# The seam between attention and the expert layer: where the first early tile's scatter, the experts' ranking and a weight block stand, and a new table of keys

## The chip, the cores and the metric

The kernel runs on one core of a Trainium2 chip. The metric is the device time in microseconds from one launch; before and after are compared on medians of several runs. TensorE is called PE, VectorE DVE, ScalarE ACT, GpSimd POOL and SyncE SP, as in the profile. Each engine works through its own queue strictly in order.

## What is computed

Linear attention for 8 batches of 8 heads, normalised per head, and behind it a layer of 8 experts of which each token uses one. A token is kept while its expert has places.

```python
kv = einsum('bhsd,bhse->bhde', k, v); out = einsum('bhsd,bhde->bhse', q, kv)    # 8 x 8 x 576 x 64
x = out / sqrt(mean(out ** 2, -1) + 1e-6) * g_norm                              # -> 4608 tokens x 512
logits = x @ w_gate; e = argmax(logits); gate = softmax(logits)[e]
h = maximum(x_e @ w1[e], 0)                                                     # 512 -> 1024
out[token] = gate * (h @ w2[e])                                                 # 1024 -> 512
```

## The kernel before

**Stages.** The attention part (about 0 to 150 us) works batch by batch: products for `kv` and for the output on PE, squares and normalisation, routing, and a write of the token rows to the tensor `x_dram`. Behind the fifth batch an early part begins: the expert that leads by then gets its weights loaded and its first 384 tokens (`EARLY`) gathered, and its first products are done beside the rest of the attention. Behind the last batch `finish` (L1343) reads the table of tokens per expert from PSUM (`read_table`, `tab_sb`, L1141), makes the row numbers of the first expert's other tokens (`sources_of_first`, `gi_rest`, L1154), and ranks the other experts by their load (`rank_steps`, L1110: compare, rank, turn, keep; the last gives `perm_i`). Then each expert has a budget of slots (704, 672, 640, 624, 592, 576, 560, 512), in tiles of 128 rows. The first expert has 320 slots left behind its early ones.

**One expert.** Its rows come by indirect gathers from `x_dram` that POOL issues (`xg`, L457), are scaled to `xm`, turned so that the 512 features lie on partitions, and split into two float16 parts (`xs`: high and low). For the first expert PE turns them (`xp`, L477), ACT and DVE copy the parts (L713, L485); for the others ACT and POOL or DVE make the pair of parts (`pair`, L491, L495) and SP issues a DMA transpose (L501). Weights are loaded by SP (`raw`, L345, four pieces of 512 KB a matrix), their maximum is taken on DVE (`am`, L361), and they are split into high and low float16 parts by ACT (L395) and DVE (L401). The hidden layer is 8 tiles `hp` of three products each (x high by w high, x low by w high, x high by w low; L551); its relu is split again (`hb`, ACT L556, DVE L559). The second product `yp` (L597) takes 24 matmuls for each tile of 128 rows: hidden high by w2 high, hidden high by w2 low, hidden low by w2 high. ACT scales it by the gate (`ysb`, L632) and POOL scatters it to the output by an indirect DMA (L637).

**The order of the work.** It is not written out by hand and not left to the compiler: while the kernel is built, class `Plan` lists the operations with assumed durations (`op`, L118) and `place` (L127) puts them on the engines one by one. Of the operations that an engine could begin soonest it takes the one with the lowest key, and of equal keys the one with the lowest number. Keys are 10 for each expert in turn (`KEY`) with small steps inside, lower for what is urgent, plus an entry for an operation's number from the table `NUDGE`, if there is one. The first plan holds the attention and early part, the second (`NUDGE[1]`) the rest. Operations are numbered as the code makes them. In the second plan 1 to 18 belong to the two early tiles that are left, 19, 26 and 33 are the three gathers of the first expert's rest (128, 128 and 64 rows), 40 to 104 its products, 105 the copy `next_i` that tells SP the second expert, 106 to 154 the second expert's rows, 155 to 228 its weights, and so on.

Of the early tokens' three output tiles the first is made in the first plan (`EARLY_TILES` = 1), scatter included; the two others (`range(EARLY_TILES, NHI)`, L1761) in the second, beside the gathers. SP's loads of the second expert's w1 wait for `next_i`, which waits for the ranking and for the three gathers:

```python
before = [op(("P", 0.12), lambda e: nc.gpsimd.tensor_copy(next_i, perm_i[0:1, 0, 1:2]),
             [early["rank"]] + sent, -KEY / 2)]
```

## Time and profile before

| | |
|---|---|
| median of 3 runs | 559.38 us (556.1, 559.38, 563.11) |
| profiled execution | 556.98 us device time, span of the instructions 555.1 us, mean granted clock 0.985 |
| busy | PE 520.3 us (94%), DVE 394.1 (71%), ACT 252.7 (46%), POOL 150.9 (27%) |
| data moved by DMA | 102.58 MB, mean 185 GB/s |

PE's share is the first thing to read: what the engine with 94% does not do is what an order of the work can still give. The busy share is a mean over two very different parts, so it has to be cut by stretch. A number in brackets such as `[2.56 <-ACT xs L713]` at a line of the timeline is the idle time of the engine before that line and what ended it.

### The profile page before, as it was taken

How to read it: one execution, taken by the hardware profiler on the slowest of the kernel's cores; microseconds unless marked ns; L12 is line 12 of the kernel's file. 1: busy time of each engine (PE TensorE's matmuls, PEld its weight loads, DVE VectorE, ACT ScalarE, POOL GpSimd, SP SyncE). 2: the span in 40 equal slices, each digit the busy share in tenths (PEclk: the TensorE clock that was granted, in tenths of full speed). 3: DMA queues.
4: the chain of work that ended last, by engine and by line, in shares of the span. 5: the costliest groups of instructions: out<-in, count | busy, mean ns of one | idle time of the engine just before them, and what ended most of it. 6: DMA issues, size and time to landing. Idle time of an engine off the chain costs nothing.

```text
span 555.1 us, 12017 instructions
## 1 busy us (share of the span) xinstructions
PE 520.3 (94%) x4599; PEld 344.2 (62%) x4599; DVE 394.1 (71%) x1041; ACT 252.7 (46%) x506; POOL 150.9 (27%) x173
## 2 busy tenths in 40 slices
PE   4989797898996999999999999999999999999995
PEld 4878695876544666546754675667468648745442
DVE  3389679989967679869868899779778785751200
ACT  1667475698413346237246282264246165212210
POOL 6001002612356553243404320220503151002011
PEclk9999798899999999999999999999999999999998
DMA  8999999744256979778619538747529341001010
GB/s 272 358 356 360 392 380 368 252 144 182 98 155 249 226 242 264 154 151 266 159 49 322 144 92 280 139 144 259 142 65 305 115 119 38 1 20 58 0 40 32
DMA packets 78019, 102.58 MB, mean 185 GB/s; under 512 B 43222, under 2 KB 51414, under 8 KB 76932
## 3 DMA queue, kind: packets, MB, share of 16 engines
q1 hardware_dynamic: 69600, 70.43, 43.3%
q0 software_dynamic: 7776, 31.30, 16.0%
q8 instruction: 38, 0.62, 0.5%
q14 instruction: 25, 0.20, 0.1%
q10 hardware_dynamic: 580, 0.02, 0.1%
HBM read 73.13 MB, written 20.61 MB: 169 GB/s over the span
## 4 chain that ended last, share of the span: by engine, by line
PE 19%; issue 18%; DMA 11%; DVE 3%; POOL 1%; ACT 1%; POOLq 0%; DVEq 0%
DMA out_dram<-ysb,si 11%; PE hp L551 11%; PE yp L597 6%; DVE am L361 2%; PE yp L612 1%; ACT w2h L395 1%; POOL xg L457 1%; DVE hb L559 1%; POOL out_dram L637 0%; POOL gt L472 0%; POOLq L1740 0%; POOLq L637 0%; DVE xm L465 0%; ACT hb L556 0%; DVE w2l L401 0%
## 5 line engine op out<-in xcount | busy, mean ns | idle before, releaser
L551 PE MATMUL hp<-xs,w1h 128*128 128x320 f16 (+6 forms) x896 | 134.6, 300 | 5.7 <-ACT xs L713 2.6
L597 PEld LDWEIGHTS <-hb 128*128 128x128 f16 x840 | 81.2, 98 | 93.4 <-issue 0.7
L597 PE MATMUL yp<-w2h,hb 128*128 128x512 f16 x544 | 127.1, 379 | 0.3 <-ACT ysb L632 0.2
L551 PEld LDWEIGHTS <-w1h 128*128 128x128 f16 x960 | 93.3, 98 | 46.9 <-issue 7.8
L637 POOL DMA_INDIRECT out_dram<-ysb,si x41 | 46.3, 1130 | 238.1 <-ACT ysb L632 180.8
L361 DVE TENSOR_REDUCE am<-raw 128x1 f32<-128x512 f32 x120 | 75.3, 677 | 12.5 <-DMA raw<-in_moe_w_dram 12.4
L556 ACT ACTIVATE hb<-hp 128x320 f16<-128x320 f32 (+7 forms) x64 | 40.6, 636 | 84.8 <-PE hp L551 70.9
L559 DVE SCALAR_TENSOR_TENSOR hb<-hp,hb 128x320 f16<-128x320 f32 (+7 forms) x64 | 47.2, 737 | 35.8 <-ACT hb L556 35.6
L551 PE MATMUL hp<-xs,w1l 128*128 128x320 f16 (+6 forms) x448 | 71.5, 300 | 0.0
L632 ACT ACTIVATE ysb<-yp,ysc 128x512 f32<-128x512 f32 (+5 forms) x40 | 27.4, 684 | 94.2 <-PE yp L597 90.9
L597 PE MATMUL yp<-w2l,hb 128*128 128x512 f16 x272 | 64.7, 379 | 0.0
L551 PEld LDWEIGHTS <-w1l 128*128 128x128 f16 x480 | 46.9, 98 | 19.4
L457 POOL DMA_INDIRECT xg<-x_dram,gi x35 | 37.1, 1061 | 34.5 <-DVE xm L465 19.8
L861 PE MATMUL op<-kv_bd,qt 128*128 128x144 f32 x256 | 44.2, 316 | 1.6 <-ACT qt L713 1.1
L401 DVE SCALAR_TENSOR_TENSOR w2l<-raw,sw,w2h 128x512 f16<-128x512 f32 x64 | 44.8, 743 | 0.5 <-ACT w2h L395 0.4
L401 DVE SCALAR_TENSOR_TENSOR w1l<-raw,sg,w1h 128x512 f16<-128x512 f32 x64 | 45.0, 746 | 0.0
L491 ACT CAST pair<-xm 128x512 f16<-128x512 f32 (+5 forms) x35 | 21.3, 615 | 46.1 <-DVE xm L465 24.1
L395 ACT ACTIVATE w1h<-raw,sg 128x512 f16<-128x512 f32 x60 | 38.8, 711 | 7.0 <-DVE sg L390 7.0
L395 ACT ACTIVATE w2h<-raw,sw 128x512 f16<-128x512 f32 x62 | 40.1, 713 | 1.0 <-DVE sw L331 1.0
L861 PEld LDWEIGHTS op<-kv_bd,qt 128*128 128x128 f32 x256 | 37.8, 210 | 3.8 <-ACT qt L713 1.8
L772 PE MATMUL a<-v_sb,k_sb 64*64 64x64 f32 x576 | 23.6, 233 | 9.2 <-DMA v_sb<-in_v_dram 7.4
L772 PEld LDWEIGHTS a<-v_sb,k_sb 64*64 64x64 f32 x576 | 20.7, 145 | 12.9 <-issue 11.6
(250 smaller groups left out, 634.6 us busy)
## 6 DMA issues: line engine op xcount, KB each, us to landing
raw<-in_moe_w_dram SPq DMA_DIRECT2D x64, 512.0 KB
k_sb<-in_k_dram SPq DMA_DIRECT2D x16, 576.0 KB
v_sb<-in_v_dram SPq DMA_DIRECT2D x16, 576.0 KB
x_dram<-o_sb POOLq DMA_DIRECT2D x8, 1152.0 KB
q_sb<-in_q_dram SPq DMA_DIRECT2D x16, 512.0 KB
x_dram<-o_sb POOLq DMA_DIRECT2D x8, 144.0 KB
q_sb<-in_q_dram SPq DMA_DIRECT2D x32, 32.0 KB
out_dram<-ysb,si POOLq DMA_INDIRECT x41
```

The lines of the kernel that those rows point to most:

```text
L361: nc.vector.tensor_reduce(out=am()[:, p:p + 1], in_=raw[:, sl(p)], axis=AX.X, op=ALU.max, apply_absolute_value=True)
L395: nc.scalar.activation(wh[:, sl(p)], raw[:, sl(p)], AF.Copy, scale=z["s"])
L401: nc.vector.scalar_tensor_tensor(out=wl[:, sl(p)], in0=raw[:, sl(p)], scalar=z["s"], in1=wh[:, sl(p)], op0=ALU.mult, op1=ALU.subtract)
L457: nc.gpsimd.indirect_dma_start(out=self.xg[i][0:n], out_offset=None, in_=x_dram[0:self.rows, :], in_offset=bass.IndirectOffsetOnAxis(ap=se ...
L551: nc.tensor.matmul(self.view(hp)[:, u], lhsT=w[:, c, j * P:(j + 1) * P], rhs=x[:, c, u * hw:(u + 1) * hw], start=(t == 0 and c == 0), stop ...
L556: nc.scalar.activation(self.out(self.hh, j), self.view(hp), AF.Relu)
L559: nc.vector.scalar_tensor_tensor(out=self.out(self.hl, j), in0=self.view(hp), scalar=0.0, in1=self.out(self.hh, j), op0=ALU.max, op1=ALU.s ...
L597: nc.tensor.matmul(yp[0:n, 0:DM], lhsT=h[:, j, o:o + n], rhs=w[:, j, :], start=(m == 0), stop=(m == len(self.terms) - 1))
L632: nc.scalar.activation(self.ysb[0:n], yp[0:n, 0:DM], AF.Copy, scale=self.ysc[0:n, i:i + 1])
L637: nc.gpsimd.indirect_dma_start(out=out[:, :], out_offset=bass.IndirectOffsetOnAxis(ap=self.sidx[0:n, col:col + 1], axis=0), in_=ysb[0:n], ...
L772: nc.tensor.matmul(banks[g].t[rows[u], half * D:(half + 1) * D], lhsT=kh.t[rows[g], u, c * D:(c + 1) * D], rhs=vh.t[rows[g], u, c * D:(c + ...
L861: nc.tensor.matmul(y, lhsT=qt.t[:, i * P:(i + 1) * P], rhs=kv2[:, half * HH + i], start=True, stop=True)
```

## The change

Four edits and a new table. (1) `second` gets a list `kept`: the scatter of the first early tile is not issued in the first plan but kept, and issued in the second with key -5, behind the three gathers of the first expert's rest (`first_sent`). Two empty operations stand in its place, so that the numbers of the others stay. (2) `finish` lets the copy of the experts' counts and the four steps of the ranking depend on `early["cut"]`, the operation that makes `gi_rest`. (3) `Gemm2` gets `low_last`, set for the early expert's tiles: the block hidden high by w2 low comes third instead of second, and `second` names the dependences in that order (`r < 0`). (4) `NUDGE[1]` is replaced, 35 entries by 397. The table of the first plan stays.

```diff
@@ -80,10 +80,46 @@
-    {3: 0.6, 26: 0.6, 99: -8.8, 110: 0.7, 149: -7.4, 289: 2.9, 377: 8.6, 436: -5, 478: 0.6, 506: -2.6, 572:
-     6.1, 590: 1.6, 594: 5.7, 633: 3.6, 678: 6.1, 691: 12.4, 716: 9.4, 726: 3.2, 783: 2.3, 795: 4.8, 809:
...
+    {10: -4.3, 36: -0.3, 57: 4.2, 91: -3.2, 99: -7.1, 102: 0.2, 108: 1.4, 109: 1.4, 110: 1.2, 111: 1.4, 112:
...
+     144: 1.4, 145: 1.4, 146: 1.4, 147: 1.4, 148: 1.4, 149: 1.4, 150: 1.4, 151: 1.4, 152: 1.4, 153: 7.5, 154:
+     7.5, 155: 7.5, 156: 7.5, 157: 7.5, 158: 7.5, 159: 5.2, 160: 5.2, 161: 5.2, 162: 5.2, 163: 5.2, 164: 5.2,
+     165: -2.2, 166: 5.2, 167: 7.5, 168: 7.5, 169: 7.5, 170: 7.5, 176: 6.1, 177: 6.1, 178: 6.1, 179: 6.1, 180:
...
+     224: -18.2, 232: -5.3, 233: 1.7, 259: 8.4, 261: 2.4, 263: -1.3, 274: 0.9, 373: 1.9, 374: -2.9, 377: 8.6,
+     383: -2.9, 399: -2.5, 448: -0.1, 455: 1.2, 457: -1.5, 495: 2.2, 503: -1.5, 506: -0.9, 510: 1.9, 511: 1.9,
...
+     -1.7, 808: 2.4, 823: -3.5, 836: 5.6, 840: 8, 858: -2.6, 861: -3.4, 862: -3.4, 863: -3.4, 864: -3.4, 865:
...
+     1445: -1.8, 1455: -1.3, 1463: -0.3, 1467: 0.3, 1468: 0.7, 1496: -5.6, 1500: 1.5, 1501: -12.3, 1524: 2.8,
+     1543: -0.8, 1547: -5.8, 1556: -6.9, 1564: -6.9, 1565: -6.9, 1566: -6.9, 1567: -8.1, 1571: 7.9})
@@ -573,13 +609,14 @@
     class Gemm2:
 
 
-        def __init__(self, pool, ws, g, gt, sidx, s0, s1, bufs=3):
+        def __init__(self, pool, ws, g, gt, sidx, s0, s1, bufs=3, low_last=False):
             self.pool, self.g, self.gt, self.sidx, self.s0, self.bufs = pool, g, gt, sidx, s0, bufs
             self.w = [w.rearrange("p (j d) -> p j d", j=KF) for w in ws[2:4]]
             self.tiles = spans(s0, s1)
             self.ysc = pool.tile([P, NHI], F32, name="ysc")
             hh, hl = g.hh, g.hl
-            self.terms = [(h, w, j) for h, w in ((hh, self.w[0]), (hh, self.w[1]), (hl, self.w[0])) for j in range(KF)]
+            pairs = [(hh, self.w[0]), (hh, self.w[1]), (hl, self.w[0])]
+            self.terms = [(h, w, j) for h, w in (pairs[::2] + pairs[1:2] if low_last else pairs) for j in range(KF)]
 
         def scales(self, scale):
             c0 = 0
@@ -1080,12 +1117,12 @@
         writes.append(ws)
         lasts[b] = ws + [ent, acc]
 
-    def count(dst, key):
+    def count(dst, key, behind=None):
 
         cp = misc[:, 64:64 + E]
         o = op(("T", 0.05), lambda e: nc.tensor.matmul(cp, lhsT=ones16, rhs=tot_acc, start=True, stop=True), accs[-1:], FIRST)
         readers.setdefault("acc", []).append(o)
-        return op(("V", 0.1), lambda e: nc.vector.tensor_copy(dst, cp), [o], key)
+        return op(("V", 0.1), lambda e: nc.vector.tensor_copy(dst, cp), [o, behind], key)
 
     def distinct(cnt):
         d = sm.tile([P, E], F32, name="dist")
@@ -1259,7 +1296,7 @@
             lows.append(op(("V", 0.61), lambda e, i=i, xp=xp: st["rows"].low(i, xp.t), [a], low, (), (xp, hold)))
         return st, hold, fetched, (gates, highs, lows)
 
-    def second(r, st, hh, hl, w2, scaled, hid, w_hold, sl_hold, s0, s1, bank, tiles=range(NHI), key=None):
+    def second(r, st, hh, hl, w2, scaled, hid, w_hold, sl_hold, s0, s1, bank, tiles=range(NHI), key=None, kept=None):
 
         key = KEY * r if key is None else key
         urgent = key - KEY
@@ -1277,8 +1314,9 @@
                         st["g2"].products(i, yp.t, c, c + 4)
 
                     js = range(c % KF, c % KF + 4)
-                    after = [(hl if c >= 2 * KF else hh)[j] for j in js] + [scaled, o]
-                    after += [w2[KF <= c < 2 * KF][j] for j in js] if w2 else []
+                    block = (0, 2, 1)[c // KF] if r < 0 else c // KF
+                    after = [(hl if block == 2 else hh)[j] for j in js] + [scaled, o]
+                    after += [w2[block == 1][j] for j in js] if w2 else []
                     o = op(("T", 0.86), product, after, k, (yp,), (hid, w_hold))
             else:
                 yt = new("ysb")
@@ -1303,9 +1341,16 @@
                 yh.t = st["g2"].out(i, yp.t)
 
             o = op(("A", 0.58), out_, [o], urgent, (yh,), (yp,))
+            if kept is not None:
+                kept.append((o, lambda e, i=i, yh=yh: st["g2"].write(i, yh.t)))
+                o = op(("S", 0.01), None, o if isinstance(o, list) else [o], key)
+                o = op(("S", 0.01), None, [o], key)
+                continue
             o = op(("P", 1.05), lambda e, i=i, yh=yh: st["g2"].write(i, yh.t), [o], key, (), (yh, sl_hold))
             o = op(("D", 0.73), None, [o], key, (), (yh,))
         return o
+
+    kept_writes = []
 
     def early_products():
         st = early["st"] = {}
@@ -1331,12 +1376,12 @@
             hl.append(op(("V", 0.07 + EARLY / 960), lambda e, j=j, hp=hp: st["g1"].low(j, hp.t), [a], LOW, (), (hp,)))
 
         def scales(e):
-            st["g2"] = Gemm2(ep, wsets[0], st["g1"], early["x"]().gt, early["si"], 0, EARLY, 2)
+            st["g2"] = Gemm2(ep, wsets[0], st["g1"], early["x"]().gt, early["si"], 0, EARLY, 2, True)
             st["g2"].scales(y_scale(*[early["z", i]["e"] for i in range(2)]))
 
         early["scaled"] = op(("V", 1.2), scales, gates + hh[:1] + list(early["w", 1][0].values()), LOW)
         second(-1, st, hh, hl, early["w", 1], early["scaled"], Hold(None), Hold(None), Hold(None), 0, EARLY,
-               ("op", lambda: bank("op")), range(EARLY_TILES), LOW + 2)
+               ("op", lambda: bank("op")), range(EARLY_TILES), LOW + 2, kept_writes)
 
     cnt_all = cst.tile([P, E], F32, name="cnt_all")
 
@@ -1355,9 +1400,9 @@
         early["cut"] = op(("V", 0.65), cut, [t], key)
         early["sources"] = op(("V", 0.2), lambda e: sources(), [t], key + 0.1)
         early["cut2"] = op(("V", 0.8), cut2, [t], key + 0.3)
-        o = count(cnt_all, key)
+        o = count(cnt_all, key, early["cut"])
         for long, f in rank_steps(cnt_all):
-            o = op(("V", long), lambda e, f=f: f(), [o], key + 0.2)
+            o = op(("V", long), lambda e, f=f: f(), [o, early["cut"]], key + 0.2)
         early["rank"] = o
 
     tiles = {0: load(0)}
@@ -1751,6 +1796,7 @@
            range(EARLY_TILES, NHI))
     st, xs_hold, sent, (gates, xh, xl) = rows(lambda: (early["gi0"], None), EARLY, BUDGET[0], N, [early["cut"]], -KEY, -KEY / 2,
                                               mo, None, lambda: psx.tile([P, 512], F32, tag="x", name="xp"), new("xs"), BM)
+    first_sent = sent
     args = (lambda st=st: st["rows"], xh, xl, gates, xs_hold, lambda: early["si0"], Hold(None), None, zs, w_holds, EARLY,
             BUDGET[0])
     for r in range(E):
@@ -1771,6 +1817,9 @@
             steps, o = plan_rest(), early["later"]
             for _ in range(71):
                 o = op(("V", 0.2), lambda e: next(steps, None), [o], key + 1)
+    for o, write in kept_writes:
+        o = op(("P", 1.05), write, (o if isinstance(o, list) else [o]) + first_sent, -KEY / 2)
+        op(("D", 0.73), None, [o], -KEY / 2)
     order = ExitStack()
     order.enter_context(tc.manual_schedule(engines={getattr(mybir.EngineType, e) for e in MANUAL}))
     plan.emit()
```

## Rows read from the trace of the kernel before

**Rows 1.** Windows: busy us of each engine by stretch, granted clock, DMA share, GB/s.
```profile
0.00:140.00 140.00, 117.94 (x1829) 101.87 (x1830) 105.40 (x374) 90.33 (x239) 33.09 (x45) 0.95 0.89 307
140.00:168.00 28.00, 27.75 (x159) 14.55 (x158) 20.98 (x82) 7.87 (x15) 14.46 (x15) 1.00 0.39 127
168.00:182.00 14.00, 9.69 (x68) 6.63 (x68) 11.61 (x26) 5.08 (x11) 9.02 (x12) 1.00 0.70 236
182.00:548.40 366.40, 364.89 (x2546) 221.16 (x2543) 256.12 (x561) 148.78 (x241) 93.36 (x101) 1.00 0.51 144
548.40:555.10 6.70, 0.02 (x1) 0.00 (x0) 0.00 (x0) 0.69 (x1) 0.97 (x1) 0.75 0.07 23
```

**Rows 2.** Timeline, PE, 155 to 179: start, us, instruction, [idle before <-what ended it].
```profile
165.10 0.65 PE L477 MATMUL xp<-ident,xm 128*128 128x128 f32 x4
...
166.55 0.46 PE L477 MATMUL xp<-ident,xm 64*128 64x64 f32 x4
166.94 1.04 PE L597 MATMUL yp<-w2h,hb 128*128 128x512 f16 x4
170.53 2.08 PE L551 MATMUL hp<-xs,w1h 128*128 128x320 f16 x12 [2.56 <-ACT xs L713]
...
174.98 1.25 PE L551 MATMUL hp<-xs,w1h 128*128 128x320 f16 x8 [0.74 <-DVE am L361]
...
177.69 1.25 PE L551 MATMUL hp<-xs,w1h 128*128 128x320 f16 x8 [0.91 <-DVE hb L559]
```

**Rows 3.** Timeline, DVE, 151 to 159.
```profile
153.17 0.16 DVE L1092 SCALAR_TENSOR_TENSOR dist<-cnt_all,desc 128x8 f32<-128x8 f32 x1
...
156.23 0.20 DVE L1134 TENSOR_SCALAR perm_i<-perm 128x8 int32<-128x8 f32 x1
...
156.84 0.44 DVE L1154 TENSOR_SCALAR gi_rest<-mine_g 128x6 int32<-128x6 f32 x1
```

**Rows 4.** Timeline, POOL, 149 to 175.
```profile
156.23 1.07 POOL L637 DMA_INDIRECT out_dram<-ysb,si  x1 [5.61 <-DVE tab_sb L1141]
158.15 1.03 POOL L457 DMA_INDIRECT xg<-x_dram,gi_rest  x1 [0.86 <-issue]
159.49 0.94 POOL L457 DMA_INDIRECT xg<-x_dram,gi_rest  x1 [0.30 <-issue]
160.73 0.97 POOL L457 DMA_INDIRECT xg<-x_dram,gi_rest  x1 [0.30 <-issue]
161.69 0.18 POOL L1762 COPY next_i<-perm_i 1x1 int32<-1x1 int32 x1
```

**Rows 5.** Timeline, ACT, 154 to 175: the copies behind the last two turns.
```profile
169.62 0.86 ACT L713 CAST xs<-xp 128x512 f16<-128x512 f32 x2 [5.24 <-remote]
```

**Rows 6.** Timeline, SP's queue, 160 to 204: us from the first issue to the last.
```profile
163.09 5.02 SPq L345 DMA_DIRECT2D raw<-in_moe_w_dram  x4
...
182.03 1.63 SPq L345 DMA_DIRECT2D raw<-in_moe_w_dram  x3
```

**Rows 7.** Windows of the stretches around the gathers, columns as in rows 1.
```profile
155.00:163.00 8.00, 7.77 (x40) 3.82 (x38) 4.94 (x26) 0.69 (x1) 5.15 (x6) 1.00 0.34 98
163.00:171.60 8.60, 6.04 (x37) 3.29 (x36) 4.58 (x9) 3.12 (x6) 5.32 (x6) 1.00 0.95 318
```

**Rows 8.** Timeline, DVE, 162 to 179: a row scaling, a piece of w1, a low part.
```profile
164.36 0.69 DVE L465 TENSOR_TENSOR xm<-xg 128x512 f32<-128x512 f32 x1 [1.38 <-DMA xg<-x_dram,gi_rest]
...
173.25 1.28 DVE L361 TENSOR_REDUCE am<-raw 128x1 f32<-128x512 f32 x2 [0.80 <-DMA raw<-in_moe_w_dram]
174.45 0.48 DVE L559 SCALAR_TENSOR_TENSOR hb<-hp,hb 128x320 f16<-128x320 f32 x1
```

**Rows 9.** Timeline, PE, 147 to 156: the first early tile's second block.
```profile
151.57 1.03 PE L597 MATMUL op<-w2l,hb 128*128 128x512 f16 x4
```

**Rows 10.** The second expert's rows: PE's wait, and line 501's transposes (ns, min/median/max).
```profile
199.69 1.16 PE L551 MATMUL hp<-xs,w1h 128*128 128x336 f16 x7 [0.16 <-DMA xs<-pair]
...
L501 SPq DMA_TRANSPOSE xs<-pair x6: 1177/1299/3492, 176.1 to 197.2; - x6
```

33 rows, old and new, of the table NUDGE are left out of this document.

## The prediction

> **What bounds the kernel now.** I read the busy table by stretch first [rows 1]. It cuts the profiled execution (span 555.1 us, device time 556.98 us) where the kernel changes its work. What PE does not do is 22.1 us in the attention part (0 to 140), 0.25 us from 140 to 168, 4.31 us from 168 to 182, 1.51 us in the 366.4 us of the eight experts, and 6.7 us after the last product, 34.8 us in all. From 182 on PE works 364.89 of 366.40 us at the full granted clock, with DVE at 70% and ACT at 41%: nothing there gets shorter by more than 1.5 us unless products are dropped, and none is. The change acts from the end of the routing (about 150) on. The instructions before it are the same, so the 22.1 us stay, and so does the tail of 6.7 us, which is the last output, its scatter and the end of the program. What it can reach is 0.25 + 4.31 + 1.51 = 6.1 us.
>
> Then I read the PE timeline over the seam [rows 2]. The products of the two early tiles that are left cover the wait for the first expert's other 320 rows until 167.98. Behind them PE stands 2.56 us for `xs`, then 0.74 us and 0.91 us: 4.21 of the 4.31 us. The DVE and POOL timelines [rows 3, 4] show what led there: the row numbers `gi_rest` are done at 157.28, the scatter of the first early tile takes POOL from 156.23 to 157.30, the first gather starts at 158.15, two more at 159.49 and 160.73.
>
> The reader is to see next that the 2.56 us are not the lateness of the gathers. The last two turns on PE end at 165.75 and 167.01 [rows 2]; ACT, idle, starts the copies that wait for them at 169.62 after 5.24 us, and the releaser is only called "remote" [rows 5]. The rows lay turned in PSUM for 3.9 and 2.6 us before ACT heard of it. In the same stretch SP needs 5.02 us to issue the four loads of the second expert's w1, where three loads at 182.03 take 1.63 us [rows 6], and the DMA engines are 95% busy [rows 7]. What held the event up no view shows; it coincides with these loads beside the gathers.
>
> **The scatter moved.** It leaves POOL's queue ahead of the first gather and comes behind the third and behind the `next_i` copy, which has the same key and a lower number. Today the first gather starts 0.86 us behind the scatter's end; the second and third start 0.30 us behind the end of the one before [rows 4]. So 0.56 us go if that distance is the scatter's, none if a first gather needs it anyway. Also, `gi_rest` takes 0.44 us beside the scatter, and the same kind of operation that begins with the scatter, `perm_i`, 0.20 us [rows 3]: 0.24 us more. From 0 to 0.8 us, and I take 0.8, because the distance is seen only at the gather that stands behind the scatter. What is queued behind the scatter in its new place are the second expert's gathers: 1.07 + 0.30 us later, less 0.8, so about 0.6 us later. Their cover is named below.
>
> **The order of the first expert's gathers.** The old keys pushed operation 26, the second gather (128 rows), behind operation 33, the third (64 rows), by +0.6; the new table has no entry for 26. The 128 rows then come 1.24 us earlier (159.49 against 160.73), the 64 rows as much later. The larger tile's row scaling, at 164.36 [rows 8], ends the chain today, so the last turn can come up to 1.2 us sooner. It is worth nothing while ACT waits for the event, so I take 0 with 1.2 as the other end (it lies within the 2.56).
>
> **The experts' order moved behind the row numbers.** Nine small DVE operations, the first `dist` at 153.17, the last `perm_i` at 156.23 [rows 3], 0.16 and 0.20 us, about 9 x 0.2 = 1.8 us together, now follow `gi_rest`; the two that stood between the table and `gi_rest` free some 0.1 us, which I leave out. Their result is then there at about 157.0 + 1.8 = 158.8, or 159.2 if the making of `gidx_tab`, an operation like `gi_rest`, goes first. The first reader, `next_i`, runs at 161.69, or 160.9 when it moves with the gathers [rows 4]: hidden by 1.7 us. Without that cover the loads of w1 would come later by what is missing. The gathers' descriptors are now written while these operations run: today's three gathers take 1.03, 0.94 and 0.97 us [rows 4], so I set a gather beside them 0.1 us dearer, and none lies on the path while the event sets it.
>
> The Trainium skill, SBUF — State Buffer, "SBUF: two separate sides", says that POOL cannot write the descriptors of such a DMA while DVE runs a copy that holds the port pair they share. By that each gather could wait for one of these short operations; with their 0.2 us, three gathers would give back 0.6 of the 0.8 us, and the time would be 0.6 us higher. The rows bear out little of it: the 0.1 us between today's gathers.
>
> **w2's low block last.** The same 24 products, in another order. PE starts the old second block at 151.57 with no idle before it [rows 9] and has 0.25 us idle from 140 to 168 [rows 1], so nothing waits for a low part today, and the new order takes nothing away: 0. The cover is PE's own queue; where a low part came late, PE would stand for as long as it is late.
>
> **The other keys.** Most of the 397 entries shift whole runs of operations together (108 to 152 by +1.4, 176 to 216 by +6.1, 510 to 573 by +1.9, 861 to 924 by -3.4 or +0.5), which leaves the order inside a run as it is. Counted through the code, 155 to 207 are the loads, maxima and splits of the second expert's weights: they go behind its rows, from which they were one or two units apart already. The trace of before cannot show the new order. Its bounds: all 1.51 us of idle in the experts' part gone, against a stall at the second expert as worked out in the last rival. I take 0.4, a quarter of the gain, since the shifted runs keep most orders as they are.
>
> **The seam's sum.** The w1 loads follow `next_i`, which follows the three gathers, so the whole stretch of the held-up event moves with the first gather: 0.8 us. For the two smaller gaps: DVE waits 0.80 us for a piece of w1 at 173.25 and the hidden tile's low part is queued behind it on DVE [rows 8], which is the 0.74 us of PE. Those loads start 0.8 us earlier, but the scatter's 128 x 512 x 4 = 262 KB now fall into the stretch with 95% busy DMA and 318 GB/s instead of the one with 34% [rows 7]; 262 KB / 318 GB/s = 0.82 us. So from -0.8 to +1.65, and I take the middle, 0.4.
>
> Gain: 0.8 + 0 + 0 + 0.4 + 0.4 = 1.6 us, 556.98 - 1.6 = 555.4 on the profiled execution. That one lies 2.4 us under the median of the runs shown (559.38, from 556.1 to 563.1), so on the median's scale 557.8.
>
> **Rivals.** *The event is on time* (0.22): the loads come apart from the gathers, the 2.56 us go, the smaller gaps shrink with them and the keys give their 1.51. For: everything else the first product needs is ready by 167.5. Against: loads and gathers move together. At most 4.21 + 1.51 = 5.7 us, 553.7.
>
> *The gain is handed back at the second expert* (0.20). Its first product waits 0.16 us at 199.69 for the turned rows [rows 10]: they are just in time today. If PE arrives 1.6 us sooner and the rows, whose gathers go 0.6 us later, do not, the wait grows by what was won: 559.4, no change. For: the six row tiles are turned by transposes on SP that take 1.18 us at best and 3.49 us at worst [rows 10], at the pace of the DMAs and not of PE. Against: these gathers are issued by about 168.5, and the first transpose comes only at 176.1. The Trainium skill, DMA: Bandwidth & Descriptors, "Issuing engines are not separate DMA queues", speaks for this rival: what one queue starts earlier runs on the same 16 engines as the rest. The 95% of [rows 7] agrees.
>
> *Slower* (0.13). One mechanism: the second expert's transposes. The new keys let the last of its row tiles go behind the w2 loads (operation 153 at +7.5 against +6.1 on loads one unit up), and the gathers come later. The median transpose takes 1.30 us, the slowest, 3.49 us [rows 10]; w2's loads are issued from 182.03 on [rows 6]. If two more tiles are turned at the slow pace beside these loads, the rows are 2 x 2.19 = 4.4 us later. The 0.16 us wait shows no slack, so PE stands these 4.4 us: 559.4 + 4.4 = 563.8. It decides once the last tile is turned later than today; the gain of 1.6 us is then gone as well.
>
> **The numbers.** My forecast has 0.45. The cases run from 553.7 to 563.8; the runs of before alone spread 3.5 us to either side. I take 552.0 to 562.5: it holds the forecast and the first two rivals, and leaves out the third and a little for the spread of the runs, 2 in 10. A measurement of this kernel tells 2% from no change, 11.2 us. Faster by that is nearly twice what PE idles where the change acts: 0.02. Slower needs the last rival's stall at three of the seven later experts: 0.04. Within 2%: 0.94.
>
> **What would show it.** In the profile after: the first gather at about 157.4 instead of 158.15 and the scatter behind `next_i`; the 128-row gather second; ACT's `xs` copies at about 168.8 with "remote" before them, or at 165 to 167 (first rival); the product on `xs` at about 169.7. For the second rival, the wait at 199.7 grows as the one at 170 shrinks. For the third, it grows beyond. I am wrong in kind if the attention part's 22.1 us move, or if the experts' part has more than 5 us of PE idle at several places.

## The result: 0.5 to 0.9% slower

| kernel | median of its runs | before beside it | ratio, 95% interval |
|---|---|---|---|
| changed kernel | 564.84 us (20 runs) | 560.15 us (20) | 1.0089 [1.0066, 1.0112] |
| changed kernel, second series (after_again) | 559.66 us (11) | 557.83 us (28) | 1.0045 [1.0023, 1.0068] |
| changed kernel, third series (after_third) | 564.40 us (12) | 560.24 us (23) | 1.0050 [1.0013, 1.0087] |

The forecast was 557.8 us, 1.6 under the 559.38 us of the three runs of before that it went by; the change costs 2 to 5 us instead. Each series stands beside runs of before on its own chip, and every ratio below is to before in the same series. The ratios leave out a few slow executions and are not simply quotients of the medians. The profile recorded with the first series (568.87 us) is the longest of its twenty runs. That of the second (559.66 us) is equal to its median, so the seam is read there.

First the cut by stretch, from the first series' profile. Columns as in [rows 1]: PE, PEld, DVE, ACT, POOL, granted clock, DMA share, GB/s.

```profile
0.00:140.00 140.00, 117.07 (x1820) 100.69 (x1821) 106.19 (x371) 89.56 (x238) 32.97 (x45) 0.95 0.88 304
140.00:168.00 28.00, 26.06 (x155) 14.04 (x153) 21.13 (x81) 9.35 (x18) 11.40 (x12) 1.00 0.34 109
168.00:182.00 14.00, 10.75 (x61) 6.36 (x60) 9.00 (x26) 2.43 (x6) 7.30 (x9) 0.88 1.01 381
182.00:548.40 366.40, 360.22 (x2517) 219.22 (x2516) 259.45 (x565) 149.74 (x243) 90.26 (x104) 0.99 0.47 138
```

The attention part idles as before (22.9 us against 22.1). The loss is behind it: PE idles 1.94 us from 140 to 168, where it was 0.25, and 6.18 us from 182 to 548.40, where it was 1.51; the granted clock is 0.88 and 0.99, where it was 1.00.

PE's waits in the second series (timeline; here the matmul `tab` ends at 153.26, 2.5 us earlier than in the profile of before, so times are best taken from there):

```profile
160.06 0.63 PE L513 MATMUL xp<-ident,xm 128*128 128x128 f32 x4 [1.24 <-issue]
161.93 0.66 PE L513 MATMUL xp<-ident,xm 128*128 128x128 f32 x4 [0.38 <-DVE gt L508]
...
173.34 1.25 PE L587 MATMUL hp<-xs,w1h 128*128 128x320 f16 x8 [2.48 <-DVE p2t L365]
...
179.17 2.29 PE L587 MATMUL hp<-xs,w1h 128*128 128x320 f16 x8 [2.41 <-DVE hb L595]
201.96 2.30 PE L587 MATMUL hp<-xs,w1h 128*128 128x336 f16 x15 [0.22 <-DMA xs<-pair]
233.48 0.60 PE L634 MATMUL yp<-w2h,hb 128*128 128x512 f16 x2 [0.48 <-ACT hb L592]
```

The 2.56 us of [rows 2] are gone, and the first expert's first product comes 14.2 us behind `tab` instead of 14.8. In place of 2.56 + 0.74 + 0.91 = 4.21 us stand 1.24 + 0.38 + 0.17 (a third wait of that kind) + 2.48 + 2.41, together 6.67 us. From 178.99 to 182.40 the clock is granted at its lower level, which takes 1.7 us more: the eight products at 179.17 last 2.29 us, those at 173.34 1.25. The profiles of the first and third series show the same waits, 5.62 and 5.60 us in all and divided otherwise (3.25 and 0.67 us, 3.10 and 0.72, for 2.48 and 2.41), with 3.41 us at the lower clock in each.

What stands in front of the 2.48 us, in DVE's timeline of the same execution:

```profile
169.90 1.28 DVE L397 TENSOR_REDUCE am<-raw 128x1 f32<-128x512 f32 x2 [1.21 <-DMA raw<-in_moe_w_dram]
171.10 0.68 DVE L501 TENSOR_TENSOR xm<-xg 128x512 f32<-128x512 f32 x1
...
172.03 0.69 DVE L397 TENSOR_REDUCE am<-raw 128x1 f32<-128x512 f32 x1
172.80 0.49 DVE L595 SCALAR_TENSOR_TENSOR hb<-hp,hb 128x320 f16<-128x320 f32 x1
```

And in ACT's timeline:

```profile
171.81 0.62 ACT L527 CAST pair<-xm 128x512 f16<-128x512 f32 x1 [3.48 <-DVE xm L501]
172.34 0.76 ACT L592 ACTIVATE hb<-hp 128x320 f16<-128x320 f32 x2
```

What stands in front of the 2.41 us, in ACT's timeline:

```profile
177.64 0.62 ACT L527 CAST pair<-xm 128x512 f16<-128x512 f32 x1 [4.55 <-POOL xm L501]
178.17 0.76 ACT L592 ACTIVATE hb<-hp 128x320 f16<-128x320 f32 x2
```

And in front of that row scaling, in POOL's timeline:

```profile
174.02 1.02 POOL L674 DMA_INDIRECT out_dram<-ysb,si  x1 [3.74 <-DVE y L367]
175.51 1.01 POOL L493 DMA_INDIRECT xg<-x_dram,gi  x1 [0.27 <-POOL gt L508]
176.54 1.07 POOL L501 TENSOR_TENSOR xm<-xg 128x512 f32<-128x512 f32 x1
```

The low part `hb` of the first hidden tile, which PE needs to go on, stands on DVE behind three maxima of w1 and a row scaling of the second expert; one of the maxima waits for a load to land. In [rows 8] it stood behind two. The high part of the same tile, from which the low part is made, is late as well: ACT has it in its queue behind a pair copy that waits 3.48 us for that row scaling, and ends it at 172.77, where the low part on DVE starts at 172.80. So two queues hold the tile up at once, and freeing one alone could not have ended the wait. The relu of the third hidden tile then stands on ACT behind a copy for the second expert that waits 4.55 us for POOL, which had a scatter in front. None of this is work for the product that waits: it is the order in the queues.

The first series' profile has one stall more, 4.01 us at 235.5, with the clock at its lower level for 6.83 us from 238.5. Again the relu is queued on ACT, behind copies that wait for transposes (ACT's timeline, first series):

```profile
232.26 0.62 ACT L527 CAST pair<-xm 128x512 f16<-128x512 f32 x1 [4.97 <-DMA xs<-pair]
237.61 0.62 ACT L527 CAST pair<-xm 128x512 f16<-128x512 f32 x1 [4.73 <-DMA xs<-pair]
238.13 1.34 ACT L592 ACTIVATE hb<-hp 128x672 f16<-128x672 f32 x2
```

In the second series this wait is 0.48 us, in the profile of the third (an execution of 573.36 us) 5.91 us. It is a place where the changed order is close to stalling, not a fixed price.

### The profile page after: what moved, and what is told of

It reads as the page before. It is cut to its first block, busy times and chain, and to the rows that moved or that the text cites. A ratio compares the mean times of both kernels' runs of the same rounds, so it can differ in the third digit from the quotient of the medians.

```text
span 567.1 us, 12013 instructions
## 1 busy us (share of the span) xinstructions
PE 525.4 (93%) x4599; PEld 345.2 (61%) x4599; DVE 395.8 (70%) x1042; ACT 253.1 (45%) x506; POOL 145.8 (26%) x172
## 5 line engine op out<-in xcount | busy, mean ns | idle before, releaser
L674 POOL DMA_INDIRECT out_dram<-ysb,si x41 | 48.0, 1171 | 248.0 <-ACT ysb L669 177.9
L634 PE MATMUL yp<-w2l,hb 128*128 128x512 f16 x272 | 66.4, 386 | 0.0
L437 DVE SCALAR_TENSOR_TENSOR w1l<-raw,sg,w1h 128x512 f16<-128x512 f32 x64 | 46.6, 773 | 0.5 <-ACT w1h L431 0.2
```

The costliest lines, as they stand in the source:

```text
L437: nc.vector.scalar_tensor_tensor(out=wl[:, sl(p)], in0=raw[:, sl(p)], scalar=z["s"], in1=wh[:, sl(p)], op0=ALU.mult, op1=ALU.subtract)
L634: nc.tensor.matmul(yp[0:n, 0:DM], lhsT=h[:, j, o:o + n], rhs=w[:, j, :], start=(m == 0), stop=(m == len(self.terms) - 1))
L674: nc.gpsimd.indirect_dma_start(out=out[:, :], out_offset=bass.IndirectOffsetOnAxis(ap=self.sidx[0:n, col:col + 1], axis=0), in_=ysb[0:n], ...
```

## The experiments

Theories. **A**: the moved scatter and the moved ranking together put the last step of the ranking (`perm_i`) behind the first row scaling on DVE, so that SP's loads for the second expert start late. **B**: the new keys alone cost it. **C**: what one wait gives back the next late thing takes, above all the second expert's turned rows. **D**: a product waits because a queue that works strictly in order has foreign work in front.

One table first. Idle and clock are from the profiled execution of each kernel: PE's idle time from the end of `tab` to the last product, how many us of that stretch had the clock at its lower level, and how far the last product's end lies behind `tab`.

| kernel | what it has of the change | ratio to before, 95% | idle | low clock | end behind `tab` |
|---|---|---|---|---|---|
| before | nothing | 1 | 6.07 | 0 | 392.66 |
| changed, first series | all | 1.0089 [1.0066, 1.0112] | 11.36 | 10.24 | 402.74 |
| after_again | all | 1.0045 [1.0023, 1.0068] | 8.72 | 3.41 | 397.24 |
| low_only | w2's low block | 1.0160 [1.0122, 1.0197] | 13.21 | 10.24 | 404.59 |
| rank_only | ranking | 1.0092 [1.0056, 1.0128] | 12.36 | 3.41 | 399.70 |
| keys_only | keys | 1.0100 [1.0056, 1.0145] | 13.50 | 10.24 | 404.60 |
| no_rank_old_keys | scatter, low block | 1.0065 [1.0036, 1.0095] | 10.19 | 0 | 397.58 |
| keys_old | all but the keys | 1.0165 [1.0122, 1.0207] | 15.51 | 6.82 | 405.59 |
| no_rank | all but the ranking | 1.0107 [1.0073, 1.0141] | 12.24 | 13.66 | 404.45 |
| no_scatter | all but the scatter | 1.0072 [1.0044, 1.0100] | 11.98 | 10.24 | 402.79 |
| keep_second | all, `perm_i` ahead of the row scaling | 1.0037 [1.0004, 1.0070] | 8.63 | 0 | 395.54 |

Each part that was tried alone (ranking, w2's low block, keys; the scatter was not) costs 0.9 to 1.6%, and the change without its scatter, its ranking or its keys 0.7 to 1.7%. The end behind `tab` grows by about the idle time plus half of the low-clock time (changed, first series: 5.29 + 5.12 = 10.4 us against 10.08).

**The keys: keys_old and keys_only.** Expected of keys_old: 

> Changed kernel with the 35 old keys instead of the 397 new ones; scatter, ranking and w2 edits stay. Theory A (the moved scatter and the moved ranking together put the last step of the ranking, `perm_i`, behind the first row scaling on VectorE, so that SP hears of the second expert 2.7 us later, and two stalls follow): the order of `perm_i` and `xm` is as in the changed kernel, `next_i` comes at about 6.8 us behind the table's matmul instead of 4, PE stalls at 174 to 178, and the time is 3 to 5 us over before. Theory B (the new keys alone cost it: eight weight loads in a row for the second expert, w2 loads ahead of the transposes for the third): time within 1 us of before.

Expected of keys_only: 

> The kernel before with nothing but the 397 new keys. Theory A: `perm_i` is early, the loads of the second expert start by 161 to 163, and the time is within 1 us of before. Theory B: 4 to 5 us over before, with the stall of 3 to 4 us at 174 to 178 and the wait of about 4 us for a split of the relu near 239.

The edit of keys_old against the changed kernel; keys_only makes the opposite exchange in the kernel before:

```diff
-    {10: -4.3, 36: -0.3, 57: 4.2, 91: -3.2, 99: -7.1, 102: 0.2, 108: 1.4, 109: 1.4, 110: 1.2, 111: 1.4, 112:
+    {3: 0.6, 26: 0.6, 99: -8.8, 110: 0.7, 149: -7.4, 289: 2.9, 377: 8.6, 436: -5, 478: 0.6, 506: -2.6, 572:
...
```

Measured 1.0165 and 1.0100: both theories miss. The new keys cost 1% where the other edits are not, and save some 0.8 to 1.2% where they are. Without the ranking's edit they save nothing: no_rank, with the new keys, is at 1.0107, no_rank_old_keys, with the old ones, at 1.0065. They are no part with a price of its own.

**One part undone or alone: no_rank, no_scatter, no_rank_old_keys, rank_only, low_only.** Expected of no_rank: 

> Changed kernel without the edit that ties count and ranking to the row numbers; scatter, w2 block and new keys stay. Theory A: `perm_i` is done before the first rows land, `next_i` follows the third gather at about 161 to 162, the stall at 174 to 178 goes and with it most of the 4.7 us: within 1 us of before. Theory B: 4 to 5 us over before as in the changed kernel.

Expected of no_scatter: 

> Changed kernel with the first early tile's scatter back in its old place, ahead of the first gather; ranking, w2 block and new keys stay. Theory A (it needs both edits): the last step of the ranking is ahead of the row scaling again, and the time is within 1 us of before. A ranking that costs by itself, because it follows the row numbers: 2 to 4 us over before with `next_i` 1 us late or more. Theory B: 4 to 5 us over before.

Expected of no_rank_old_keys: 

> Changed kernel without the ranking's edit and with the 35 old keys: the scatter behind the gathers and w2's low block last alone. If the 10 us of keys_old come from the ranking behind the row numbers (`perm_i` behind the row scaling): within 1.5 us of before. If they come from the moved scatter, which shifts the plan that the old keys were made for: 5 to 10 us over before.

Expected of rank_only: 

> The kernel before with the ranking behind the row numbers alone; here `perm_i` follows the ranking directly, ahead of the row scaling. If the ranking costs only by standing behind the row scaling: within 1.5 us of before. If the later ranking costs by itself, or by the order that the planner then makes with the old keys: 3 to 10 us over before.

Expected of low_only: 

> The kernel before with w2's low block last in the early tiles and nothing else. The prediction costed this at nothing: within 1 us of before, PE without idle from 150 to 167. If the other order of the block re-sorts the plan behind it, as the other edits did with the old keys: 3 us or more over before.

The edit of no_rank against the changed kernel; rank_only makes the opposite one in the kernel before, and the others take out or put in the hunks of the change in the same way:

```diff
-        o = count(cnt_all, key, early["cut"])
+        o = count(cnt_all, key)
         for long, f in rank_steps(cnt_all):
-            o = op(("V", long), lambda e, f=f: f(), [o, early["cut"]], key + 0.2)
+            o = op(("V", long), lambda e, f=f: f(), [o], key + 0.2)
```

By A, no_rank and no_scatter, where `perm_i` is early, had to be at before; they are at 1.0107 and 1.0072. no_rank_old_keys, 3.6 us over before, lies between the two ranges that were expected of it; rank_only, 5.1 us over, lies in the second of its own. low_only is the plainest miss of the prediction: 1.0160, 8.9 us, for an edit costed at nothing. PE has indeed no idle time between 150 and 164 beyond the 0.23 us that it has in before too; it loses 4.95 us at the second expert, and the clock with it. The same place costs 5.50 us in rank_only, 4.84 in no_scatter, 4.20 in no_rank and 4.17 in keys_only. What it is shows POOL's timeline, of no_rank first:

```profile
198.84 1.01 POOL L674 DMA_INDIRECT out_dram<-ysb,si  x1 [3.90 <-ACT ysb L669]
199.88 1.16 POOL L531 TENSOR_TENSOR pair<-xm,pair 32x512 f16<-32x512 f32 x1
```

PE in the same execution:

```profile
203.56 2.67 PE L587 MATMUL hp<-xs,w1h 128*128 128x336 f16 x9 [4.20 <-DMA xs<-pair]
```

POOL in low_only:

```profile
198.17 1.03 POOL L638 DMA_INDIRECT out_dram<-ysb,si  x1 [5.85 <-ACT ysb L633]
199.23 1.16 POOL L495 TENSOR_TENSOR pair<-xm,pair 32x512 f16<-32x512 f32 x1
```

And its PE:

```profile
202.92 3.52 PE L551 MATMUL hp<-xs,w1h 128*128 128x336 f16 x12 [4.95 <-DMA xs<-pair]
```

POOL stands 3.9 and 5.9 us for an output tile of the first expert, in order to issue its scatter; the last pair copy of the second expert, 32 rows whose input is there, is queued behind it, and its transpose and PE's product behind that. (no_scatter shows the same; in keys_only ACT's half of the copy is late too, behind an output tile in ACT's queue.) In the kernel before the same copy starts at 196.00, 40.2 us behind `tab`; here it starts 45.8 and 45.3 us behind it. Nothing in the w2 edit touches these instructions: with other dependences `place` finds other start times, and so another order.

**The pair copy and the scatter exchanged on POOL: no_rank_pair and rank_pair.** Expected of no_rank_pair: 

> The kernel no_rank with one instruction of POOL moved: the last pair copy of the second expert (32 rows) stands ahead of the second scatter of the first expert's output instead of behind it; no other engine's order changes. Theory C: the last transpose comes about 4 us earlier, the 4.20 us wait of PE at 199.4 shrinks to under 0.5, the half clock from 200.9 to 207.7 goes with it, and the time falls by 5 to 7.5 us against no_rank, to within 2 us of before. If the transposes are held up by the weight loads and not by this scatter: the wait stays over 3 us and the time stays 6 to 7 over before.

Expected of rank_pair: 

> The kernel rank_only with the first scatter of the first expert's output moved on POOL behind the last pair copy of the second expert, and ACT's half of that pair copy moved ahead of three weight splits; nothing else changes its place. Theory C (rows of the second expert late because their last pair copy is queued behind a scatter that waits for PE, and behind splits): the 5.50 us wait of PE at 200.1 falls below 2, the half clock behind it goes, and the time is 4 to 6.5 us below rank_only, within 1.5 us of before or under it. Rival (the rows are late for another reason, the ring of two pair buffers or slow transposes): the wait stays over 4 us and the time within 1.5 us of rank_only.

Operations are moved in the finished order by a small addition to `emit`: of each pair, the operation with the first number goes to the place directly ahead of that with the second, and all others stay. The first list is that of no_rank_pair (152 is the pair copy, 97 the second scatter), the second that of rank_pair (88 is the first scatter, 322 the instruction behind the copy; 151 is ACT's half of the copy, 180 a weight split):

```diff
-    def emit(self):
-        for o in self.place():
+    def emit(self, early=()):
+        order = self.place()
+        for n, m in early:
...
+    plan.emit([(152, 97)])
...
+    plan.emit([(88, 322), (151, 180)])
```

rank_pair settles the place: 1.0092 [1.0056, 1.0128] becomes 1.0024 [0.9998, 1.0049], which is 3.8 us by the ratios (the two series ran on different chips), and the 5.50 us are gone; PE does not wait there at all. In rank_only the scatter and the copy were long as well as late (POOL's timeline):

```profile
193.39 3.93 POOL L638 DMA_INDIRECT out_dram<-ysb,si  x1 [0.18 <-issue]
197.32 0.20 POOL L472 COPY gt<-xg 32x1 f32<-32x1 f32 x1
197.47 3.86 POOL L495 TENSOR_TENSOR pair<-xm,pair 32x512 f16<-32x512 f32 x1
```

What DVE did beside them:

```profile
193.69 2.72 DVE L401 SCALAR_TENSOR_TENSOR w1l<-raw,sg,w1h 128x512 f16<-128x512 f32 x4
...
197.60 2.72 DVE L401 SCALAR_TENSOR_TENSOR w1l<-raw,sg,w1h 128x512 f16<-128x512 f32 x4
```

In no_rank_pair the same move takes the 4.20 us away, but the ratio goes only from 1.0107 to 1.0084, inside both intervals: PE now waits 3.31 us at 205.57 for a low part that stands on DVE behind eight splits of w2 and two maxima. There C holds for the wait; the time cannot tell.

**`perm_i` moved: keep_second, keep_second_old, keep_second_again.** Expected of keep_second: 

> Changed kernel in which the last step of the ranking (`keep`, which writes `perm_i`) is issued from the second plan with a key ahead of all others; VectorE then writes `perm_i` ahead of the first row scaling, everything else keeps its place. Theory A (`perm_i` behind the row scaling costs the seam its stall): the loads of the second expert start about 2 us earlier, the 3.25 us wait at 174.5 and the half clock behind it shrink, and the time is 3 to 5 us below the changed kernel, 0 to 2 over before. Theory C (every stall moves to the next thing that is late, here the pair copies of the second expert, queued on POOL behind a scatter): the seam's stall goes, but a wait for the second expert's turned rows takes its place near 200, and the time stays 4 to 6 us over before.

Expected of keep_second_old: 

> keep_second with the 35 old keys instead of the 397 new ones; tells what the new keys are worth once `perm_i` stands ahead of the row scaling. If the new keys only cost: within 1 us of before. If they were fitted to the order that the other edits make: 5 to 8 us over before, where keep_second is 2 over.

```diff
-        for long, f in rank_steps(cnt_all):
+        *steps, early["keep"] = rank_steps(cnt_all)
+        for long, f in steps:
...
+    keep = early["rank"] = op(("V", long), lambda e, f=f: f(), [early["rank"]], -20 * KEY)
+    plan.ops.remove(keep)
...
+    plan.ops.append(keep)
```

(The last three lines stand in the second plan; put at its end, the operation leaves the numbers of the others as they are.)

The step that A names is real. The changed kernel, second series, DVE's timeline:

```profile
156.74 0.22 DVE L1167 TENSOR_REDUCE perm<-cmp 128x8 f32<-128x64 f32 x1
159.27 0.69 DVE L501 TENSOR_TENSOR xm<-xg 128x512 f32<-128x512 f32 x1 [2.31 <-DMA xg<-x_dram,gi_rest]
159.94 0.16 DVE L1170 CAST perm_i<-perm 128x8 int32<-128x8 f32 x1
```

And POOL's:

```profile
160.17 0.18 POOL L1808 COPY next_i<-perm_i 1x1 int32<-1x1 int32 x1 [1.23 <-DVE perm_i L1171]
```

The ranking is done at 156.96, its last step waits 2.31 us behind a row scaling for a gather, and POOL waits 1.23 us for it. In keep_second the loads start 6.7 us behind `tab` instead of 7.9. It came out at 1.0037, which looked like 3 us won; but the changed kernel's second series, on another chip, gave 1.0045. So both ran on one chip. Expected of after_again: 

> The changed kernel itself, unaltered, beside the others on one chip. Its profiled execution was the longest of its twenty, so it is open which of its stalls are there each time. If the 3.25 us at 174.5 and the 4.01 us at 235.5 are of the kernel, both come again within 1 us; if the second is of that execution, it is under 2 us and the half clock behind it is missing. Time 4 to 6 us over before.

Expected of after_third: 

> The changed kernel again, beside keep_second on one chip, because the two were only compared through different chips, and the changed kernel came out at 1.0089 and at 1.0045 of before. It should lie between 2 and 5 us over before. The stall of the seam near 17.6 us behind the table's matmul comes again (2.4 to 3.3 us); the one near 79 us behind it is between 0.5 and 4.

Expected of keep_second_again: 

> keep_second again, on the same chip as the changed kernel. Theory A (`perm_i` behind the row scaling costs 2 to 3 us): 1.5 to 3.5 us under the changed kernel. Rival (the place of `perm_i` costs nothing by itself, since the second expert's start is set by other queues, and the difference seen before was that of the chips): within 1 us of the changed kernel.

On one chip keep_second is at 1.0074 [1.0034, 1.0115] and the changed kernel at 1.0050 [1.0013, 1.0087], medians 563.47 and 564.40 us. A's 1.5 to 3.5 us do not show: by the medians keep_second is 0.9 us lower, by the ratios 1.3 us higher, and each interval is 2 us to either side. So no price of the place of `perm_i` can be told from nothing, and with no_rank and no_scatter, which cost as much with `perm_i` early, A falls as the cause. Of the expectations, the seam's wait came in all three profiles of the changed kernel (3.25, 2.48, 3.10 us); the one near 79 us behind `tab` was outside its range in the third (5.91); and the second series, 2.5 us over before, was below the expected 4 to 6. keep_second_old, at 1.0176 [1.0133, 1.0220], says of the keys what keys_old said.

**Waits taken away one by one: keep_second_hb, keep_second_act, before_hb, rank_pair_hb.** Each lets relu parts go ahead of foreign work in one queue (keep_second_act in two), by the same addition. Expected of keep_second_hb: 

> The kernel keep_second with the relu's low parts of the first expert's first two hidden tiles moved on VectorE ahead of three maxima (`am`) that wait for pieces of the second expert's w1. Theory D (in-order queue: hidden tiles wait because VectorE stands for a weight load): the waits of 2.42 us at 171.2 and 1.44 us at 177.0 shrink to under 1 us together, and the time falls by 2 to 3 us against keep_second, to before or up to 1 us under it. Theory C (handed on): the two waits shrink as said, but the second expert's rows come no earlier, PE waits the same 2 to 3 us there, and the time stays within 1 us of keep_second.

Expected of keep_second_act: 

> The kernel keep_second_hb with the relu's high parts moved on ACT ahead of the two pair copies of the second expert that wait for a row scaling. keep_second_hb lost 5 us to keep_second with a 4.06 us wait at 175.5, in which ACT's relu is queued behind such a copy. Theory D: with both queues in that order the waits at 171 and 175.5 are under 1 us together, and the time is 1 to 3 us under keep_second, near before. Theory C: the second expert's pair copies are now later, PE waits there instead, and the time is that of keep_second or more.

Expected of before_hb: 

> The kernel before with the relu's low parts of the first expert's first two hidden tiles moved on VectorE ahead of two maxima that wait for pieces of w1 and of the scales; no other engine's order changes. It takes 1.65 us of stalls out of the seam (0.74 and 0.91). Theory C (what the seam gains is handed back at the second expert, whose turned rows are just in time): the two waits go, the 0.16 us wait at 199.7 grows to 1.3 to 1.8, the time stays within 0.7 us of before. Theory that seam gains come through: 1.5 us under before.

Expected of rank_pair_hb: 

> The kernel rank_pair with one relu low part of the second expert moved on VectorE ahead of two row scalings of the third, which wait for their gathers, and of two maxima. Theory D (in-order queue): the 2.43 us wait at 218.8 and the half clock behind it go, together 3 to 4 us, the time is 0 to 2.5 us under before. If the wait moves to the next queue: within 1 us of rank_pair.

The lists, in the order keep_second_hb, keep_second_act, before_hb, rank_pair_hb. The relu parts themselves do not stand in them; what was queued ahead of them is put behind them. 163 to 170 and 373, 374 are maxima, 80 the scales, 111, 112, 119 and 120 pair copies, 340 and 348 row scalings:

```diff
+    plan.emit([(169, 80), (170, 80), (165, 166), (80, 166)])
...
+    plan.emit([(169, 80), (170, 80), (165, 166), (80, 166), (112, 118), (111, 119), (120, 126), (119, 63)])
...
+    plan.emit([(167, 80), (168, 80), (80, 169)])
...
+    plan.emit([(88, 322), (151, 180), (341, 357), (349, 357), (340, 375), (348, 375), (373, 375), (374, 375)])
```

keep_second_hb, at 1.0109 [1.0050, 1.0168], is no faster than keep_second (1.0037 and 1.0074 in its two series, on other chips), and keep_second_act, at 1.0197 [1.0154, 1.0240], is slower than it: D's time, 1 to 3 us gained, misses. For the first of the two waits D holds: 2.42 us in keep_second, 1.20 with DVE's queue free, none with ACT's free as well. So that wait was the order in these two queues. In keep_second_hb, where the wait on DVE shrinks, a longer one comes through ACT (its timeline):

```profile
177.57 0.62 ACT L534 CAST pair<-xm 128x512 f16<-128x512 f32 x1 [5.77 <-POOL xm L508]
178.10 0.76 ACT L599 ACTIVATE hb<-hp 128x320 f16<-128x320 f32 x2
```

PE in the same execution:

```profile
172.05 1.25 PE L594 MATMUL hp<-xs,w1h 128*128 128x320 f16 x8 [1.20 <-DVE hb L602]
179.53 2.03 PE L594 MATMUL hp<-xs,w1h 128*128 128x320 f16 x8 [4.06 <-DVE hb L602]
```

keep_second_act frees that queue too; PE then waits 4.37 us at 174.4 for DVE and 6.16 us at 232.9, where the first series' profile had 4.01. DVE is at work in these 4.37 us and waits for no load: a copy of 128 x 6 integers (`gi`) takes 2.87 us, from 175.09 to 177.96, while POOL issues a gather, scales rows and makes a pair copy from 174.70 to 177.93. In keep_second_hb the same copy takes 2.88 us, in the changed kernel's second series 0.15:

```profile
175.82 2.88 DVE L717 COPY gi<-gidx_tab 128x6 int32 x1
```

rank_pair_hb (1.0031 [1.0005, 1.0057]) cuts the 2.43 us of rank_pair to 1.28 and gets 2.65 us at 228.2. With no_rank_pair these are four kernels in which a wait was removed or cut and another grew in the next queue.

before_hb takes the waits of 0.74 and 0.91 us out of the kernel before; 0.49 us of them stay, and the time is the same (1.0010 [0.9985, 1.0036]). Its second expert starts 44.1 us behind `tab`, with 0.43 us of waiting for turned rows, where before starts at 43.9 with 0.16: the time is as C says, but the way is not: 0.27 us more at the second expert are not the 1.3 to 1.8 that C expected, and the clock, at its lower level for 3.41 us from 169.2 in this execution, takes about 1.7 us, more than the two waits gave. The 0.91 us of before look like those 4.37: two small DVE operations for the scales (`ysc`) take 1.52 us, where they take 0.34 in before_hb, while POOL makes a pair copy and a row scaling, and the low part that PE needs is queued behind them. That POOL holds DVE up in both is read from the times; no run takes the two apart. DVE, then POOL, in the kernel before:

```profile
175.72 1.52 DVE L588 TENSOR_SCALAR ysc<-gt,ys 128x2 f32<-128x2 f32 x2
177.16 0.47 DVE L559 SCALAR_TENSOR_TENSOR hb<-hp,hb 128x320 f16<-128x320 f32 x1
...
174.89 1.17 POOL L495 TENSOR_TENSOR pair<-xm,pair 128x512 f16<-128x512 f32 x1
176.03 1.06 POOL L465 TENSOR_TENSOR xm<-xg 128x512 f32<-128x512 f32 x1
```

before_hb also shows what the seam of the kernel before waits for. ACT's timeline:

```profile
163.30 0.59 ACT L720 CAST xs<-xp 128x512 f16<-128x512 f32 x1 [1.31 <-PE xp L484]
164.55 0.37 ACT L720 CAST xs<-xp 128x256 f16<-128x256 f32 x1 [0.67 <-PE xp L484]
```

DVE's:

```profile
166.22 1.28 DVE L368 TENSOR_REDUCE am<-raw 128x1 f32<-128x512 f32 x2 [2.42 <-DMA raw<-in_moe_w_dram]
167.41 0.68 DVE L492 TENSOR_TENSOR xs<-xp,xs 128x512 f16<-128x512 f32 x1
```

PE's:

```profile
169.07 1.11 PE L558 MATMUL hp<-xs,w1h 128*128 128x320 f16 x4 [2.50 <-DVE xs L492]
```

And SP's queue:

```profile
160.83 2.42 SPq L352 DMA_DIRECT2D raw<-in_moe_w_dram  x4
```

Up to this point the order of every engine is that of before. ACT's copies follow the turns at once, SP issues its four loads in 2.42 us, and PE still waits 2.50 us: the low part `xs` stands on DVE behind two maxima that wait for w1. The profile of before has the same two maxima there, over at 169.71, so the late copies on ACT (169.62 in [rows 5]) cost it little (DVE's timeline, before):

```profile
168.43 1.28 DVE L361 TENSOR_REDUCE am<-raw 128x1 f32<-128x512 f32 x2 [2.12 <-DMA raw<-in_moe_w_dram]
170.24 0.69 DVE L485 TENSOR_TENSOR xs<-xp,xs 128x512 f16<-128x512 f32 x1 [0.54 <-ACT xs L713]
```

The 5.24 us of [rows 5] and the 5.02 us of [rows 6] were not there in before_hb's execution, which has the same order.

No kernel here is faster than before. before_hb, which has nothing of the change, is level with it; of the kernels with a part of the change rank_pair comes nearest.

## Why the prediction was wrong, point by point

- **Where the change can act**: right. The attention part idles 22.9 us where it idled 22.1, the tail takes 7.4 us where it took 6.7; the differences lie behind the end of the routing, in the changed kernel up to the third expert.
- **The 2.56 us are the late event** [rows 2, 5]: wrong. The copies on ACT were late in that execution, but before_hb without this waits 2.50 us within the same hidden tile, for a maximum that waits for a load, and that maximum stands in DVE's queue in before as well, from 168.43 to 169.71. The rival "event on time", which had these 2.56 us in its price, happened in the changed kernel, where the first product came 0.6 us earlier behind `tab`, and paid nothing.
- **The scatter, 0.8 us**: mis-sized. The first gather starts 2.15 us behind `tab` instead of 2.39: 0.24 us, the part that the prediction had put on a faster `gi_rest`. The 0.86 us that I charged to the scatter in [rows 4] are needed anyway; with no scatter in front the first gather starts 0.95 us behind `gi_rest` (154.46 to 155.41 in the second series).
- **The order of the gathers, 0**: held. The 128-row gather comes second.
- **The ranking, hidden by 1.7 us**: the cover was not there, since the last step came to stand behind a row scaling that waits for a gather; `next_i` comes 6.9 us behind `tab`, where it was 5.9. No cost of this could be measured (keep_second_again beside the changed kernel). The 0.1 us that I set for a gather beside the short operations was not needed: the three gathers take 1.03, 0.97 and 0.92 us.
- **w2's low block, 0**: right for the product, wrong for the edit. I asked who waits for the block and not what the changed dependences do to the order of everything behind: alone it costs 1.6%; in its profile 4.95 us are a wait at the second expert and up to 3.4 the lower clock there.
- **The other keys, 0.4 us gained, "the shifted runs keep most orders as they are"**: this is the step that failed. The order inside a run stays, its place among the others does not: eight loads for the second expert in a row where [rows 6] has four, three maxima and a row scaling ahead of `hb` where two stood, two pair copies behind a scatter where one stood. PE's idle time behind `tab` grows by 2.65 us (second series) to 5.29 us (first), and 3.41 to 10.24 us are run at the lower clock, where the sum had a gain of 1.6. The 0 for w2's low block rests on the same assumption. keys_only and keys_old show that keys and edits have no separate prices, so a sum over the parts could not be right.
- **The smaller gaps, 0.4 us gained**: instead of shrinking by 0.4, the seam's waits grew from 4.21 to 6.67 us in the second series' profile (5.62 and 5.60 in the others), and the clock took 1.7 us more. The 0.91 us, which I had counted with the w1 loads, went with two `ysc` operations of 1.52 us beside POOL (0.34 in before_hb).
- **The rivals**: handing back at the second expert was looked for in before_hb, without the change, and came to 0.27 us there. The slower rival had the right place and price, 4.2 to 5.5 us for the second expert's rows in five kernels, but through another mechanism: not slow transposes beside loads (five of no_rank's six last 1.2 to 1.4 us) but a pair copy behind a scatter on POOL. In the changed kernel itself this lateness is hidden, since PE arrives late: the last transpose starts 46.2 us behind `tab`, and PE waits 0.22 us. A shorter seam would run into these rows; that this is why keep_second does not pay was not tested.
- **The sign of being wrong in kind**, more than 5 us of PE idle in the experts' part at several places: it showed in the first series' profile (6.18 us, 4.01 of them at one place), not in the second's.

What stays open: the first of the seam's two long waits is the order on DVE and ACT, as keep_second_act shows, but which of the changed orders has a price in time is not settled. Each one that was put back made room for the next, and a kernel with all queues of the seam in the old order and the change's edits was not tried.

## What to carry to other kernels

Where a planner with keys by operation number sets the order, an edit's price is not the work that it moves but the order that comes out: list the new order of every queue around the bound first, and look in it for instructions that wait (a scatter for its output, a maximum for its load) ahead of small ones that the busy engine needs. A key table fits one graph of dependences; a part of a change measured with the keys of another says nothing about the part. A wait in one profiled execution may be that execution's own: ask what else stood in its way at the same time before a price is put on it, and measure 1% effects side by side on one chip. Look too for small operations that take several times their usual duration: such a one has begun and is held up by what runs beside it, not by what stands ahead of it.

## What the runs showed of the hardware

- **DVE and POOL hold each other up.** In rank_only a scatter's issue took 3.93 us and a copy of 32 rows 3.86 us beside four DVE splits each, where such a scatter takes 1.0 and such a copy 1.16 us in no_rank; they end 0.9 and 1.0 us behind the end of their four splits. The other way round, one split in no_rank takes 2.58 us (0.74 for the next ones) beside a scatter and a pair copy on POOL, and the `gi` copy above 2.87 instead of 0.15. The Trainium skill, SBUF — State Buffer, "SBUF: two separate sides", calls the port pair that the two share an exclusive lock, held for the whole instruction. These rows agree, and show more: the one that waits waited through a whole run of the other's instructions, at a price of 1.2 to 2.9 us. The prediction asked about it for the gathers alone, where it cost nothing, and not for the seam's small DVE operations.
- **A stall can cost twice.** In or just behind waits of 1.8 to 6.2 us the clock was granted at its lower level (1.2 GHz) for 3.41 or 6.83 us: 3.41 behind the 2.41 us of after_again, 6.83 behind the 4.20 us of no_rank. Where PE works through such a stretch, that adds 1.7 or 3.4 us. It does not follow each time: the 2.56 us of before and the 2.42 us of keep_second had full clock behind them.
- **The same kernel differs from series to series by 0.4%, nearly as much as the change costs**: 1.0089, 1.0045 and 1.0050 of before, on three occasions.
